# A new order for the first head pair's steps in an attention + two-layer feed-forward kernel on one core

## Chip, cores and metric

One core of one Trainium2 chip runs the kernel. The metric is device time in microseconds (us) of one execution, median over runs. Times inside the execution are counted from the start of the profiled span.

## What is computed

The inputs are q, k, v of 2 batches, 8 heads, 768 positions and head size 64 in float32, two integers (`n_global` = 8, `n_local` = 96), and the weights of two feed-forward layers. The reference, cut to what matters:

```python
scores = (q @ k.T) / sqrt(64)                       # per batch and head
rel = pos[:, None] - pos[None, :]
keep = (pos[None, :] < n_global) | ((rel >= 0) & (rel < n_local))
dist = where(is_global & ~is_local, n_local, abs(rel))
scores = where(keep, scores - slope[h] * dist, -1e9)
a = softmax(scores)                                 # over the keys
x = (a @ v) laid out as [1536, 512]
x = leaky_relu(x @ w_in) @ w_out                    # 512 -> 2048 -> 512
out = rational(x @ w_in2) @ w_out2                  # (a0+a1h+a2h^2+a3h^3)/(1+|b0 h|+|b1|h^2)
```

## The kernel before

Most keys are masked out, so a block of 128 queries needs only its own block of keys, the block before it and the first 32 keys (the "slot", `prep_slots`, replaces the first 32 columns of the block before). Work is cut into **units**: one block of queries of one head. A head **pair** (two heads, stacked in the 128 partitions) has 12 units; unit u has block i = u // 2 and head j = u % 2. There are 8 pairs, so 96 units. Every matmul operand is split into a high and a low float32r part (`kh`/`kl`, `qh`/`ql`), so a score takes three matmuls: kh with qh, kl with qh, kh with ql.

The steps of a unit are: `scores` on TensorE into one half of a PSUM bank (`score_banks[j]`, half i % 2); `least` on VectorE (bias added, minimum taken, result `sn` and `st`); `exp` on ScalarE (`pr`); `transposes` on TensorE into `pt` (two buffers); `evacuate` on ScalarE or VectorE (`pts`); `values` on TensorE. The loop over n (line 638) writes them out by hand as a software pipeline: at n it issues scores and leasts of n, `exp` of n - 1, transposes and evacuation of n - 3, values of n - 5, and then `fillers(n)`. From n = 8 on the scores of four units are issued together every fourth n. The order of every engine is the order of this code (`manual_schedule`); each engine takes its instructions strictly in that order and waits at semaphores.

Fillers prepare the next pair. `prep_k` and `prep_q` are generators that run one step for each n: transposes on TensorE into a bank (line 324); then ScalarE takes the high part of k (line 334) or a scaled copy of q (362); then VectorE takes k's low part (336), and GpSimd splits q (364, 365); then GpSimd copies the slots (352). The banks come from `ffn.bank()`, a pool of **two** that are used in turn (line 682); a transpose into a bank waits until all that read its last contents are done. `PREP0` (line 57) says at which n these generators start during the first pair: k half 0 at 4, q half 0 at 5, k half 1 at 8, q half 1 at 9.

The first pair has its own generators q0, k0 (blocks 0 and 1) and q1, k1 (blocks 2 to 5), `prep_first_q` and `prep_first_k`, since nothing runs before them. Dummy matmuls (`keep_busy`, line 531) run on TensorE ahead of and between its first steps; `BUSY` holds their numbers. The window bias (`window_bias`) is built at the same time: for block 0 (`first`, 128 columns) and for the other blocks (256 columns), by `far` (a comparison on VectorE, then the first 32 columns), `near` and `half` (the second head's slope). Two integers read from memory (`read_ints`) are spread over the partitions by a matmul (`spread`) into `nums`.

`load_v` loads v twice: `vc` in blocks of 128, and `vp`, the same values shifted by one block with the first 32 rows replaced by the first 32 keys (three DMAs per head, on the queue of SyncE). The loads of pairs 0 and 1 stand at lines 550 to 553.

Of the kernel before, what the change touches and what calls it, by code (L numbers as in the profile page):

```python
# [8 lines left out]
F32 = mybir.dt.float32  # L9
# [3 lines left out]
AF = mybir.ActivationFunctionType  # L13
# [4 lines left out]
P = 128  # L18
# [3 lines left out]
EPS_Q = 1.0 + 1e-6  # L22
FAR = 2.56e11


@with_exitstack
def attention_moe_moe2(
# [28 lines left out]

    PREP0 = (("prep_k", 4, 0), ("prep_q", 5, 0), ("prep_k", 8, 1), ("prep_q", 9, 1))
    PREP = (("prep_k", 0, 0), ("prep_q", 1, 0), ("prep_k", 4, 1), ("prep_q", 6, 1))
# [5 lines left out]
    FIRST = 8  # L64
    BUSY = (12, 3, 8)
    XOUT_LAST = (2, 8)
# [26 lines left out]
    intf = cpool.tile([1, 4], F32, name="intf")  # L93
    num1 = cpool.tile([1, 2], F32, name="num1")
    ones = cpool.tile([1, P], F32, name="ones")
    nums = cpool.tile([P, 2], F32, name="nums")
    n_loc = nums[:, 0:1]
# [5 lines left out]
    def read_ints():  # L103
        nc.vector.tensor_copy(intf, ints)
        lo, hi = (intf.rearrange("p (j w) -> p j w", w=2)[:, :, w] for w in range(2))
        nc.vector.scalar_tensor_tensor(hi, lo, 0.0, hi, ALU.is_lt, ALU.add)
        nc.vector.scalar_tensor_tensor(num1, hi, 4294967296.0, lo, ALU.mult, ALU.add)

# [112 lines left out]
    def window_bias(bpool, rpool):  # L221
# [17 lines left out]
        def part(first):  # L239
            return slice(W2, BW) if first else slice(0, W2)  # L240

        def far(first):
            cs = part(first)
            nc.vector.tensor_scalar(mask[:, cs], dist[:, cs], n_loc, FAR, ALU.is_ge, ALU.mult)
            gs = slice(cs.start, cs.start + GW)
            nc.vector.scalar_tensor_tensor(mask[:, gs], col, n_glo, mask[:, gs], ALU.is_ge, ALU.mult)

# [10 lines left out]

        return bias, far, near, half

    def attention(wpool, w1, ffn):
        with ExitStack() as actx:
# [26 lines left out]
            class Pair:  # L289
# [20 lines left out]
                def load_v(self, heads=(0, 1)):  # L310
                    b, h0 = self.b, 2 * self.hp
                    self.vc, self.vp = v_places[self.n % 2]
                    for j in heads:
                        vs = v[b, h0 + j].rearrange("(i p) d -> p i d", p=P)
                        nc.sync.dma_start(self.vc[:, j, :, 0:D], vs)
                        nc.sync.dma_start(self.vp[GW:P, j, :, 0:D], vs[GW:P, 0 : NB - 1])
                        nc.sync.dma_start(
                            self.vp[0:GW, j, :, 0:D], v[b, h0 + j, 0:GW].unsqueeze(1).to_broadcast([GW, NB - 1, D])
                        )

                def transposed(self, raw, s):
# [210 lines left out]

            keep_busy(BUSY[0])
            bias, bias_far, bias_near, bias_half = window_bias(bpool, rpool)
            next(q0)
            read_ints()
            spread = ps.tile([P, W2], F32, tag="pt", name="spread")[:, 0:2]
            nc.tensor.matmul(spread, ones, num1, start=True, stop=True)
            next(k0)
            keep_busy(BUSY[1])  # L540
            next(q0)
            next(k0)
            nc.vector.tensor_copy(nums, spread)
            bias_far(True)
            next(q0, None)
            next(k0)
            next(k0, None)
            bias_near(True)
            bias_half(True)
            P_[1].load_k()  # L550
            P_[0].load_v((0,))
            P_[1].load_q()
            P_[0].load_v((1,))

# [32 lines left out]
            def fillers(n):  # L587
# [29 lines left out]
                for u in AHEAD_STEPS.get(n, ()):  # L617
                    ffn.h_step(u)
                if n == 0:
                    start(k1)  # L620
                    start(q1)
                if n == 1:
                    bias_half(False)
                for g in new:
# [5 lines left out]
            LV = 5  # L630
            GROUPS = {m: (m,) for m in range(0, FIRST, 2)}
            GROUPS.update({m: (m, m + 2) for m in range(FIRST, len(U), 4)})

            LEASTS = {m: (m, m + 1) for m in range(0, FIRST, 2)}
            for m in range(FIRST, len(U), 4):
                LEASTS[m], LEASTS[m + 1] = (m, m + 1), (m + 2, m + 3)
            n = 0
            while n < len(U) or running or n <= len(U) + LV + 1:

                for m in GROUPS.get(n, ()):  # L640
                    for _ in zip(unit(m).scores(), unit(m + 1).scores()):
                        pass
                    if n == 2:
                        keep_busy(BUSY[2])
                for m in LEASTS.get(n, ()):
                    unit(m).least()
                    if m == 1:
                        bias_far(False)
                        bias_near(False)
                for m in (0, 1) if n == 1 else (n - 1,):  # L650
                    if n != 2 and unit(m):
                        unit(m).exp()
                if unit(n - 3):
                    unit(n - 3).transposes()
                    unit(n - 3).evacuate()
                if unit(n - LV):
# [489 lines left out]
```

## Time and profile before

| | us |
|---|---|
| median of 3 runs (637.2 to 637.66) | 637.21 |
| the profiled execution | 637.13 |
| its span, first to last instruction | 635.3 |
| TensorE busy in the span | 626.5 |
| VectorE / ScalarE / GpSimd busy | 469.1 / 439.1 / 206.9 |

The attention takes the first 109 us or so, the feed-forward layers the rest. A row of a timeline gives the start, the duration, engine, line, operation, output and inputs with their shapes, and in brackets how long the engine was idle before it and what released it. Durations on TensorE, VectorE and ScalarE contain a fixed part that overlaps with the next instruction, so the distance from one start to the next is shorter than the duration.

### The profile page before, as it was taken

To read this page: it belongs to the slowest core of one execution; us is meant where nothing else is said; L and a number is where in the kernel's file an instruction comes from. 1 tells how busy PE (TensorE), PEld (TensorE's weight loads), DVE (VectorE), ACT (ScalarE), POOL (GpSimd) and SP (SyncE) were. 2 spreads that over 40 slices of the span, in tenths; PEclk is the share of its full clock that TensorE was granted. 3 is DMA by queue.
4 is the path that set the end of the run, shared out by engine and by line. 5 is a ranking of instruction groups with operands and counts; after the bars stand their busy time and mean duration, and the time that the engine had idled before them with its cause. 6 is when DMAs were issued, how large, how long until landed. Compare 5 with 4: busy or idle time off the path is not lost.

```text
span 635.3 us, 9655 instructions
## 1 busy us (share of the span) xinstructions
PE 626.5 (99%) x3289; PEld 527.7 (83%) x3289; DVE 469.1 (74%) x931; ACT 439.1 (69%) x831; POOL 206.9 (33%) x221
## 2 busy tenths in 40 slices
PE   8999999999999999999999999999999999999996
PEld 7999998888888888888888888888888888888884
DVE  6888888878877545456444489998777777897785
ACT  6888988768776545455444377876677888876672
POOL 3978864443443434341000012222222222112220
PEclk9999999999999999999999999999999999999999
DMA  9987742955267776765322301000033331100002
GB/s 185 222 176 174 165 113 71 311 183 182 81 200 224 229 225 202 245 191 194 99 91 90 91 29 34 1 1 1 0 102 97 101 96 48 68 21 1 2 1 72
DMA packets 80895, 73.34 MB, mean 115 GB/s; under 512 B 50948, under 2 KB 67332, under 8 KB 80836
## 3 DMA queue, kind: packets, MB, share of 16 engines
q1 hardware_dynamic: 80048, 71.12, 39.5%
q0 software_dynamic: 224, 0.92, 0.4%
q8 instruction: 28, 0.46, 0.3%
q10 hardware_dynamic: 564, 0.59, 0.3%
q14 instruction: 31, 0.25, 0.1%
HBM read 60.69 MB, written 11.93 MB: 114 GB/s over the span
## 4 chain that ended last, share of the span: by engine, by line
PE 97%; DVE 2%; ACT 0%; issue 0%; DVEq 0%
PE h L691 41%; PE y L815 21%; PE y L813 21%; PE pt L476 3%; PE sc L440 3%; PE o L498 3%; PE o L497 2%; PE h L324 1%; PE h L209 1%; PE idle L531 0%; PE o L495 0%; DVE sn L451 0%; DVE xl L215 0%; DVE ql L415 0%; DVE kl L402 0%
## 5 line engine op out<-in xcount | busy, mean ns | idle before, releaser
L691 PE MATMUL h<-xh,w 128*128 128x512 f32 x768 | 253.4, 390 | 0.0
L691 PEld LDWEIGHTS h<-xh,w 128*128 128x128 f32 x768 | 144.1, 188 | 29.8
L691 PE MATMUL h<-xl,w 128*128 128x512 f32 x384 | 149.4, 389 | 0.0
L746 POOL TENSOR_TENSOR gl<-u,gh 128x512 fp32r<-128x512 f32 x44 | 57.0, 1296 | 264.4 <-PE y L815 125.4
L813 PE MATMUL y<-gh,w 128*128 128x512 f32 x384 | 126.1, 389 | 0.0
L815 PE MATMUL y<-w,gh 128*128 128x512 f32 x384 | 125.6, 389 | 0.0
L164 POOL TENSOR_TENSOR dec<-dec,wraw 128x512 int32<-128x512 int32 x48 | 63.6, 1334 | 82.7 <-DVE wraw L151 76.3
L813 PEld LDWEIGHTS y<-gh,w 128*128 128x128 f32 x384 | 72.1, 188 | 15.1
L815 PEld LDWEIGHTS y<-w,gh 128*128 128x128 f32 x384 | 72.1, 188 | 15.0
L691 PEld LDWEIGHTS h<-xl,w 128*128 128x128 f32 x384 | 72.2, 188 | 14.5
L815 PE MATMUL y<-w,gl 128*128 128x512 f32 x192 | 75.1, 391 | 0.0
L813 PE MATMUL y<-gl,w 128*128 128x512 f32 x192 | 74.7, 389 | 0.0
L716 DVE TENSOR_TENSOR gl<-h,gh 128x512 fp32r<-128x512 f32 x48 | 33.0, 688 | 51.9 <-ACT gh L715 51.9
L715 ACT ACTIVATE gh<-h 128x512 fp32r<-128x512 f32 x48 | 28.6, 596 | 59.5 <-PE y L813 53.4
L768 ACT ACTIVATE h<-h 128x512 f32<-128x512 f32 x48 | 28.7, 597 | 52.2 <-PE h L691 52.1
L711 DVE SCALAR_TENSOR_TENSOR h<-h,g 128x512 f32<-128x512 f32 x48 | 33.3, 694 | 26.0 <-ACT g L710 25.7
L756 DVE SCALAR_TENSOR_TENSOR w<-w,epsq,h 128x512 f32<-128x512 f32 (+1 forms) x49 | 36.4, 744 | 21.0 <-ACT h L780 20.4
L710 ACT ACTIVATE g<-h 128x512 f32<-128x512 f32 x48 | 28.7, 598 | 30.0 <-PE h L691 29.7
L465 ACT ACTIVATE pr<-sn,st 128x256 f32<-128x256 f32 (+1 forms) x96 | 47.3, 495 | 0.6 <-DVE st L451 0.5
L770 DVE SCALAR_TENSOR_TENSOR w<-h,coef,w 128x512 f32<-128x512 f32 x48 | 35.9, 749 | 16.0 <-ACT w L769 15.8
L815 PEld LDWEIGHTS y<-w,gl 128*128 128x128 f32 x192 | 36.0, 188 | 8.5 <-POOL gl L746 1.1
L813 PEld LDWEIGHTS y<-gl,w 128*128 128x128 f32 x192 | 36.0, 188 | 7.4
(126 smaller groups left out, 1119.2 us busy)
## 6 DMA issues: line engine op xcount, KB each, us to landing
wraw<-in_moe_w_in_dram SPq DMA_DIRECT2D x24, 512.0 KB, 4.6
wraw<-in_moe_w_out_dram SPq DMA_DIRECT2D x24, 512.0 KB, 4.6
scratch<-dec SPq DMA_DIRECT2D x32, 256.0 KB, 5.3
wf<-scratch SPq DMA_DIRECT2D x16, 512.0 KB, 3.5
w<-in_moe_w_in_dram SPq DMA_DIRECT2D x8, 512.0 KB, 4.3
w<-in_moe_w_out_dram SPq DMA_DIRECT2D x8, 512.0 KB, 5.3
vc<-in_v_dram SPq DMA_DIRECT2D x16, 192.0 KB, 3.2
qkraw<-in_q_dram SPq DMA_DIRECT2D x6, 512.0 KB, 3.6
```

The source lines that it names most:

```text
L164: nc.gpsimd.tensor_tensor(ti, ti, self.c, ALU.add)
L465: nc.scalar.activation(self.pr[:, :w], self.sn[:, :w], AF.Exp, bias=self.least_at, scale=-1.0,)
L691: nc.tensor.matmul(h, wt[:, m, c * P : (c + 1) * P], xs[:, c, cs], start=c == 0 and n == 0, stop=c == NK - 1 and n == 2,)
L710: nc.scalar.activation(g, h, AF.Copy)
L711: nc.vector.scalar_tensor_tensor(h, h, 0.01, g, ALU.mult, ALU.max)
L716: nc.vector.tensor_tensor(gl, h, gh.bitcast(F32), ALU.subtract)
L746: (nc.gpsimd if on_pool else nc.vector).tensor_tensor(gl, g, gh.bitcast(F32), ALU.subtract)
L756: nc.vector.scalar_tensor_tensor(ow[:, cs], ow[:, cs], epsq, oh2[:, cs], ALU.add, ALU.mult)
L768: nc.scalar.activation(h2, h, AF.Square)
L770: nc.vector.scalar_tensor_tensor(w0, h2, coef[:, 7:8], w0, ALU.mult, ALU.add)
L813: nc.tensor.matmul(ys[d], wt[:, m, ds_], gs, start=st, stop=sp)
L815: nc.tensor.matmul(ys[d], gs[:, ds_], wt[:, m, :], start=st, stop=sp)
```

## The change

The first pair's steps, up to n = 5, leave the loop and are written out in a new order. The transposes of k0 come before `spread`. The second halves k1 and q1 start between the first score matmuls, the scores of units 2, 3 and of 4, 5 follow one another, and the leasts of 2 to 5 come after both. The mask `far` becomes one `Relu` on ScalarE, (dist + 1 - n_local) * 2^38 cut at zero, and the first 32 columns are a step of their own (`glob`) on VectorE. All of the first pair's v is loaded before pair 1's k and q; for this pair the shifted copy is not loaded but copied from `vc` by GpSimd (`copy_v`). Pair 1's first k and q halves start at n = 6 and 7 instead of 4 and 5. The dummies become 16, 3, 3, 5 and 3 instead of 12, 3 and 8.

```diff
-FAR = 2.56e11
+FAR = 2.0**38
...
-    PREP0 = (("prep_k", 4, 0), ("prep_q", 5, 0), ("prep_k", 8, 1), ("prep_q", 9, 1))
+    PREP0 = (("prep_k", 6, 0), ("prep_q", 7, 0), ("prep_k", 8, 1), ("prep_q", 9, 1))
...
-    BUSY = (12, 3, 8)
+    BUSY = (16, 3, 3, 5, 3)
...
+        nc.vector.tensor_scalar(num1[:, 2:3], num1[:, 0:1], -FAR, FAR, ALU.mult, ALU.add)
...
         def far(first):
-            cs = part(first)
-            nc.vector.tensor_scalar(mask[:, cs], dist[:, cs], n_loc, FAR, ALU.is_ge, ALU.mult)
-            gs = slice(cs.start, cs.start + GW)
-            nc.vector.scalar_tensor_tensor(mask[:, gs], col, n_glo, mask[:, gs], ALU.is_ge, ALU.mult)
+            cs = slice(W2, BW) if first else slice(GW, W2)
+            nc.scalar.activation(mask[:, cs], dist[:, cs], AF.Relu, bias=nums[:, 2:3], scale=FAR)
+
+        def glob(first):
+            if first:
+                m = mask[:, W2 : W2 + GW]
+                nc.vector.scalar_tensor_tensor(m, col, n_glo, m, ALU.is_ge, ALU.mult)
+            else:
+                nc.vector.tensor_scalar(mask[:, 0:GW], col, n_glo, FAR, ALU.is_ge, ALU.mult)
...
-                        nc.sync.dma_start(self.vp[GW:P, j, :, 0:D], vs[GW:P, 0 : NB - 1])
+                        if self.n > 0:
+                            nc.sync.dma_start(self.vp[GW:P, j, :, 0:D], vs[GW:P, 0 : NB - 1])
...
+                def copy_v(self, j):
+                    for r in (slice(GW, 2 * GW), slice(2 * GW, P)):
+                        d = self.vp[r, j, :, 0:D]
+                        z = zeros[r].unsqueeze(1).to_broadcast([r.stop - r.start, NB - 1, D])
+                        nc.gpsimd.tensor_tensor(d, self.vc[r, j, 0 : NB - 1, 0:D], z, ALU.add)
...
             next(q0)
+            next(k0)
             read_ints()
...
             nc.tensor.matmul(spread, ones, num1, start=True, stop=True)
-            next(k0)
             keep_busy(BUSY[1])
             next(q0)
             next(k0)
+            next(q0, None)
             nc.vector.tensor_copy(nums, spread)
+            next(k0)
             bias_far(True)
-            next(q0, None)
-            next(k0)
             next(k0, None)
+            bias_glob(True)
             bias_near(True)
             bias_half(True)
+            P_[0].load_v()
             P_[1].load_k()
-            P_[0].load_v((0,))
             P_[1].load_q()
-            P_[0].load_v((1,))
...
-                if n == 0:
-                    start(k1)
-                    start(q1)
-                if n == 1:
-                    bias_half(False)
...
-            n = 0
+            begun = together(0)
+            next(begun)
+            next(k1)
+            list(begun)
+            next(q1)
+            next(k1)
+            bias_far(False)
+            unit(0).least()
+            unit(1).least()
+            list(together(2))
+            next(q1)
+            next(k1)
+            next(k1, None)
+            next(q1, None)
+            unit(0).exp()
+            unit(1).exp()
+            bias_glob(False)
+            bias_near(False)
+            bias_half(False)
+            for step, _ in enumerate(together(4)):
+                if step == 0:
+                    keep_busy(BUSY[2], P // 2)
+            for m in range(2, 6):
+                unit(m).least()
+            P_[0].copy_v(0)
+            P_[0].copy_v(1)
+            n = 3
...
                 if unit(n - 3):
                     unit(n - 3).transposes()
+                    if n in (4, 5):
+                        keep_busy(BUSY[n - 1], P // 2)
                     unit(n - 3).evacuate()
```

## Rows read from the trace of the kernel before

**Rows 1.** The page's chain that ended last, shares of the span by engine.
```profile
PE 97%; DVE 2%; ACT 0%; issue 0%; DVEq 0%
```
**Rows 2.** TensorE per microsecond: us, busy (instructions), granted clock, DMA share, GB/s.
```profile
10.00:11.00 1.00, 0.76 (x4) 1.00 1.32 220
...
13.00:14.00 1.00, 1.00 (x11) 1.00 1.37 209
```
**Rows 3.** Timeline of TensorE, the dummies and the first transposes.
```profile
3.85 0.41 PE L531 MATMUL idle<-warm 128*128 128x256 f32 x1
4.06 0.63 PE L383 MATMUL h<-ident,qr 128*128 128x128 f32 x2
5.11 0.44 PE L383 MATMUL h<-ident,kr 128*128 128x128 f32 x2
...
8.64 1.22 PE L531 MATMUL idle<-warm 128*128 128x256 f32 x8
```
**Rows 4.** Timeline of ScalarE in the first pair.
```profile
5.58 0.38 ACT L400 ACTIVATE kh<-h 128x256 fp32r<-128x256 f32 x1 [0.47 <-PE h L383]
...
8.11 0.58 ACT L400 ACTIVATE kh<-h 128x512 fp32r<-128x512 f32 x1
...
10.01 0.28 ACT L482 ACTIVATE pts<-pt 128x128 f32<-128x128 f32 x1
```
**Rows 5.** Timeline of VectorE in the first pair.
```profile
7.17 0.29 DVE L451 CUSTOM_DVE_ANT_0 sn<-sc,bias 128x128 f32<-128x128 f32 x1
...
8.27 0.48 DVE L250 SCALAR_TENSOR_TENSOR bias<-dist,nums,mask 128x256 f32<-128x256 f32 x1
8.90 0.42 DVE L451 CUSTOM_DVE_ANT_0 sn<-sc,bias 128x256 f32<-128x256 f32 x1
...
10.46 0.68 DVE L415 SCALAR_TENSOR_TENSOR ql<-h,qh 128x512 fp32r<-128x512 f32 x1
```
**Rows 6.** Instructions by line and shape in 0 to 20 us: busy, mean ns | idle before.
```profile
L465 ACT ACTIVATE pr<-sn,st 128x128 f32<-128x128 f32 x2 | 0.7, 395 | 0.3 <-DVE st L451 0.3
L244 DVE TENSOR_SCALAR mask<-dist,nums 128x128 f32<-128x128 f32 x1 | 0.3, 286 | 0.0
L413 ACT ACT_TABLE_LOAD x1 | 1.3, 1283 | 2.1 <-issue 2.1
```
**Rows 7.** Timeline of TensorE from unit 4's scores to unit 12's.
```profile
11.20 0.39 PE L440 MATMUL sc<-kh,ql 64*128 64x256 f32 x2 [0.21 <-DVE ql L415]
...
13.13 0.38 PE L440 MATMUL sc<-kh,qh 64*128 64x256 f32 x2
...
14.84 0.39 PE L440 MATMUL sc<-kh,qh 64*128 64x256 f32 x2
...
16.41 0.50 PE L324 MATMUL h<-ident,kr 128*128 128x128 f32 x3
...
19.29 0.28 PE L440 MATMUL sc<-kh,ql 64*128 64x128 f32 x2
```
**Rows 8.** The chain that ended last, in order of time, around 12.6 us.
```profile
12.56 0.12 issue
```
**Rows 9.** Timeline of VectorE around unit 8's least.
```profile
14.48 0.55 DVE L336 TENSOR_TENSOR kl<-h,kh 128x384 fp32r<-128x384 f32 x1
...
15.85 0.42 DVE L451 CUSTOM_DVE_ANT_0 sn<-sc,bias 128x256 f32<-128x256 f32 x1 [0.49 <-PE sc L440]
```
**Rows 10.** Timeline of GpSimd, preparation of pair 1.
```profile
15.11 0.97 POOL L352 TENSOR_TENSOR kl<-kl,zeros 128x288 fp32r<-128x288 f32 x2 [0.76 <-DVE kl L336]
16.04 0.83 POOL L364 TENSOR_TENSOR qh<-qt,zeros 128x384 fp32r<-128x384 f32 x1
16.95 1.00 POOL L365 TENSOR_TENSOR ql<-qt,qh 128x384 fp32r<-128x384 f32 x1
```
**Rows 11.** Timelines of GpSimd and VectorE where both read SBUF.
```profile
25.14 1.34 POOL L365 TENSOR_TENSOR ql<-qt,qh 128x384 fp32r<-128x384 f32 x1
...
24.78 0.83 DVE L151 SCALAR_TENSOR_TENSOR wraw<-wraw 128x512 int32<-128x512 int32 x1
```

More of the change, by code (lines that the diff above doesn't have):

```diff
@@ L93, in attention_moe_moe2 @@
     intf = cpool.tile([1, 4], F32, name="intf")
-    num1 = cpool.tile([1, 2], F32, name="num1")
+    num1 = cpool.tile([1, 3], F32, name="num1")
     ones = cpool.tile([1, P], F32, name="ones")
-    nums = cpool.tile([P, 2], F32, name="nums")
+    nums = cpool.tile([P, 3], F32, name="nums")
     n_loc = nums[:, 0:1]
@@ L106, in read_ints @@
         nc.vector.scalar_tensor_tensor(hi, lo, 0.0, hi, ALU.is_lt, ALU.add)
-        nc.vector.scalar_tensor_tensor(num1, hi, 4294967296.0, lo, ALU.mult, ALU.add)
+        nc.vector.scalar_tensor_tensor(num1[:, 0:2], hi, 4294967296.0, lo, ALU.mult, ALU.add)
+        nc.vector.tensor_scalar(num1[:, 2:3], num1[:, 0:1], -FAR, FAR, ALU.mult, ALU.add)
     coef = cpool.tile([P, 8], F32, name="coef")
@@ L257, in half @@
                 nc.scalar.activation(bias[:, 1, cs], bias[:, 0, cs], AF.Copy, scale=0.5)
-        return bias, far, near, half
+        return bias, far, glob, near, half
     def attention(wpool, w1, ffn):
@@ L533, in attention @@
             keep_busy(BUSY[0])
-            bias, bias_far, bias_near, bias_half = window_bias(bpool, rpool)
+            bias, bias_far, bias_glob, bias_near, bias_half = window_bias(bpool, rpool)
             next(q0)
+            next(k0)
             read_ints()
-            spread = ps.tile([P, W2], F32, tag="pt", name="spread")[:, 0:2]
+            spread = ps.tile([P, W2], F32, tag="pt", name="spread")[:, 0:3]
             nc.tensor.matmul(spread, ones, num1, start=True, stop=True)
-            next(k0)
             keep_busy(BUSY[1])
@@ L630, in attention, with together @@
             LV = 5
-            GROUPS = {m: (m,) for m in range(0, FIRST, 2)}
+            GROUPS = {m: (m,) for m in range(6, FIRST, 2)}
             GROUPS.update({m: (m, m + 2) for m in range(FIRST, len(U), 4)})
-            LEASTS = {m: (m, m + 1) for m in range(0, FIRST, 2)}
+            LEASTS = {m: (m, m + 1) for m in range(6, FIRST, 2)}
             for m in range(FIRST, len(U), 4):
                 LEASTS[m], LEASTS[m + 1] = (m, m + 1), (m + 2, m + 3)
-            n = 0
+            def together(m):
+                return zip(unit(m).scores(), unit(m + 1).scores())
+            begun = together(0)
[25 more added lines that the diff above has]
+            n = 3
             while n < len(U) or running or n <= len(U) + LV + 1:
                 for m in GROUPS.get(n, ()):
-                    for _ in zip(unit(m).scores(), unit(m + 1).scores()):
+                    for _ in together(m):
                         pass
-                    if n == 2:
-                        keep_busy(BUSY[2])
                 for m in LEASTS.get(n, ()):
                     unit(m).least()
[L647 to L652, printed above, removed]
+                if unit(n - 1):
+                    unit(n - 1).exp()
                 if unit(n - 3):
                     unit(n - 3).transposes()
+                    if n in (4, 5):
+                        keep_busy(BUSY[n - 1], P // 2)
                     unit(n - 3).evacuate()
```

## The prediction

> **What bounds the kernel now.** I read the chain of work first: 97% of the span is TensorE [rows 1], so an edit counts only by what it does to TensorE's own order. Then TensorE's busy time by microsecond: up to 13 us it has holes (0.76 us of work between 10 and 11), from 13 us on it is full, at a granted clock of 1.00 [rows 2]. So all that the change can give or take lies ahead of some point near 14 us, and behind that point each microsecond of delay is passed on whole to the end. My mark is the start of the first grouped score run, unit 8, at 14.84 [rows 7]. From there both kernels give TensorE the same list. The new time is the old one, plus the shift of this mark, plus any wait that is new behind it.
>
> In the timelines of single engines I then looked for what TensorE waits for ahead of the mark. The last real wait is for ql of the second q half, which VectorE does from 10.46 to 11.14 and which releases the score matmuls at 11.20 [rows 5, 7]. A shorter stop follows at 12.56, 0.12 us in the chain under "issue", ahead of pair 1's first q transposes [rows 8]: nothing on an engine, so by elimination their load.
>
> **The dummies.** The twelve run 0.21 us apart (3.85 to 4.06), as 256 columns do at 1.2 GHz; eight later ones take 1.22 us, 0.13 apart, the 2.4 GHz level [rows 3]. Four more ahead of the first transposes cost 4 x 0.21 = 0.84, or 4 x 0.13 = 0.52 if the clock has risen by then. I take 0.84, since two transposes that start at 4.06 still take 0.63 where two at 5.11 take 0.44 [rows 3]. The q transposes start at 4.90 and end at 5.34.
>
> **First halves.** ScalarE's qh follows at 5.36 and kh about 0.3 behind it. With 0.38 for kh [rows 4] kh is done at 6.03; before it was done at 5.58 + 0.38 = 5.96 [rows 4], since k's transposes stood behind `spread`. So what the dummies cost, the new place of `spread` pays back: level within 0.1. The mask moves to ScalarE: 0.395 by the nearest row with 128 columns (an exponential with a pointer bias) against 0.286 on VectorE [rows 6], two handovers more, and `nums` is copied behind ql. I get the first least at 7.57 instead of 7.17 [rows 5]. `num1`'s third column is one tiny VectorE step, 0.2 at most, hidden by the dummies.
>
> **Second halves.** Their k transposes start behind the first two score matmuls at 6.47 and take some 0.6, so kh of four blocks starts on ScalarE at 7.10 instead of 8.11 [rows 4]. The 224-column Relu, about 0.47, stands between it and qh, which waits for its own transposes until 8.1 in any case. Then ql takes 8.72 to 9.40 instead of 10.46 to 11.14 [rows 5]. This is the gain of the change: the scores of units 4 and 5 are complete at 9.6 instead of 11.6, 2 us earlier.
>
> **Where it goes.** The second bias is now queued behind kl and ql on VectorE. `near` of 256 columns started at 8.27 and takes 0.48 [rows 5]; now it starts at 9.52 and ends at 10.0, or 10.15 with the contention below. Unit 2's least starts at 10.0 to 10.2 instead of 8.90 [rows 5]. ScalarE then does half, the exponential of unit 2, and only behind it unit 0's evacuation: 10.9 to 11.05 instead of 10.01 [rows 4]. It takes 0.28, and the third transposes need the `pt` buffer that it frees, so they start at 11.2 to 11.4. The five dummies lie inside this wait and are free. The three behind the transposes (0.13 each, 0.4) are on the path, and so are unit 0's values. Scores of unit 6 start at 12.35 to 12.5 instead of 13.13 [rows 7]: 0.7 ahead, the stop at 12.56 [rows 8] included.
>
> From there to the mark it was 14.84 - 13.13 = 1.71 [rows 7]. Now pair 1's first k and q transposes lie in this stretch as well; three of them last 0.50 [rows 7], of which some 0.17 overlaps with what follows, so 0.33 each and 0.66 for both. The mark comes to 12.43 + 1.71 + 0.66 = 14.80, a shift of -0.04. The bounds are wide: -0.5 with a clock that rises early and no contention, +0.6 with a late bias.
>
> **Behind the mark: a bank.** The transposes of pair 1 take two banks in turn. Before, k half 0 used one at n = 4 and k half 1 came back to it at n = 8. Now k half 0 uses it at n = 6. Its last reader is VectorE's kl, two steps after the start, so at n = 8, and k half 1's transposes are issued in that same n = 8, right behind it. On VectorE kl stands behind the leasts of units 8 and 9. Unit 8's least started at 15.85, which is 1.01 behind the mark, when the whole grouped run was done [rows 7, 9]; two leasts 0.35 apart bring kl to mark + 1.70; it takes 0.55 [rows 9], so the bank is free at mark + 2.25, with the handover 2.31. TensorE is there at 16.41 - 14.84 = mark + 1.57 [rows 7]. New wait: 0.74, with nothing to hide it, since TensorE keeps its order. Queued behind it are all of TensorE's later steps. If least waited only for its own unit's matmuls, it would be 0.35 shorter; 0.4 is my lower end.
>
> GpSimd says nearly the same in another way: pair 1's kl slots, qh and ql take 0.97 + 0.83 + 1.00 and stood in one unbroken line from 15.11 to 17.95, ahead of their use at 19.29, mark + 4.45 [rows 7, 10]. Behind a kl that ends at mark + 2.25 they end at mark + 5.1. So if the bank didn't hold TensorE, ql would, for about 0.6. The two don't add: with the bank's 0.74 the use moves to mark + 5.2.
>
> **Moved under cover.** The loads: SyncE now issues v first; for pair 1's q that is 464 KB instead of 352 KB ahead, 112 KB at 220 GB/s [rows 2], 0.5 us later than its 12.6, some 0.4 to 1.0 before its use at 14.4. If that cover is gone, each tenth is paid at n = 7. The two shifted loads (120 KB each) that are left out make later transfers earlier, and none of those is waited for behind 14 us, where TensorE is full [rows 2]. `copy_v`: four GpSimd instructions of 320 columns, about 0.7 each between the rows of 288 + 96 and 384 columns [rows 10], 2.8 us from 8.7 to 11.5; unit 2's values want them near 14, and GpSimd's next work comes at 14.6.
>
> **Contention.** `copy_v` runs while `near` reads two operands from SBUF. In this trace GpSimd's ql takes 1.34 beside a VectorE step with two SBUF operands (24.78, 0.83) and 1.00 elsewhere [rows 10, 11]: 0.34 more. I put half of that, 0.15, on `near`; the ends are 0 and a whole copy, 0.7. The Trainium skill's page "SBUF — State Buffer", section "SBUF: two separate sides", says that VectorE and GpSimd share a port pair which one of them holds for its whole instruction while the other blocks. By that rule `near` could wait out a whole copy and the time would be that of the second rival; the 0.34 above shows a part of one only.
>
> **Sum.** 637.13 (the profiled execution, span 635.3 and 1.8 around it) - 0.04 + 0.74 = 637.83; the median lies 0.08 above the profiled one, so 637.9.
>
> **Rivals.** *The front gains more.* If the second bias were no bound (a least of unit 2 not much later than before), the third transposes could follow the dummies at 10.8 and the mark would come at 14.2; with the shorter wait of 0.4 that is 637.13 - 0.6 + 0.4 = 636.9, and 636.3 if neither bank nor GpSimd held anything. For it speaks the 2 us gained on ql; against it that ScalarE takes unit 2's exponential ahead of the evacuation in program order. Even this stays inside 0.2%.
>
> *Slower.* GpSimd's copies hold `near`: from the point where `near` starts inside a copy (8.7 to 11.5, and it starts at 9.5) and waits for its end, 0.55 more than I put. ScalarE's half, unit 2's exponential and all behind follow, and the mark shifts by +0.5; with the bank 637.13 - 0.04 + 0.55 + 0.74 + 0.1 = 638.5. For it speaks the 1.34 [rows 11]; against it that this is a third of what it would need.
>
> *The Relu brings a table.* The trace has one table load, 1.28 [rows 6], ahead of the attention; if Relu needed another, one more would stand ahead of unit 0's exponential and 0.9 of it would reach the mark: 638.8. No row of before has a Relu. The skill's page "ScalarE: Activation LUTs", section "Table sets", says that cheap functions such as relu are in every set; by that there is no second load and 637.9 stands.
>
> **Chances.** Forecast (bank wait with a mark near 14.8): 0.60, 637.4 to 638.4. Front gains more: 0.20, 636.3 to 637.3. Copies hold `near`: 0.16. Table: 0.04. A measurement of this kernel can tell about 0.2%, 1.27 us, from no change. Faster by more than that needs the mark below 13.6 with no wait behind it: 0.06. Slower than 638.48: most of the last two cases and the upper edge of the first, 0.18. The rest, 0.76, is within. The range runs from 636.5 to 638.7.
>
> **What would show it.** In the new profile: q's first transposes at 4.9 and kh done near 6.0; ql of the second half near 9.4; unit 2's least after 10; the third transposes released by ScalarE's evacuation near 11.3; unit 8's scores between 14.3 and 15.4; and then pair 1's second k transposes (line 324's loop) idle for 0.4 to 0.75, released by VectorE's kl. No such idle time would say that the bank reasoning is wrong; unit 8's scores before 14 that the bias chain is. A second table load, or `near` over 0.9 us, would name the slow rivals. The forecast falls if the time leaves 636.5 to 638.7.

## The result and the profile after

| | before | after |
|---|---|---|
| median, us | 637.21 | 642.27 |
| lowest to highest of eight executions | 636.53 to 638.35 | 639.16 to 643.52 |
| the profiled execution | 637.13 | 642.23 |
| its span | 635.3 | 640.4 |

The change costs 5.1 us: the ratio after to before is 1.0074 (95% interval 1.0057 to 1.0091). The forecast was 637.9 in a range of 636.5 to 638.7, a loss of 0.7 that could not be told from no change. The measured loss is seven times as large and lies outside the range.

TensorE in the new profile, first the steps that the prediction named (start us, duration us, engine, line, operation, shapes; in brackets the idle time before it and what released it):

```profile
4.91 0.63 PE L396 MATMUL h<-ident,qr 128*128 128x128 f32 x2
5.33 0.63 PE L396 MATMUL h<-ident,kr 128*128 128x128 f32 x2
...
10.37 0.46 PE L489 MATMUL pt<-ident,pr 128*128 128x128 f32 x2
10.76 0.85 PE L544 MATMUL idle<-warm 64*128 64x256 f32 x5
12.57 0.53 PE L489 MATMUL pt<-ident,pr 128*128 128x128 f32 x2 [0.96 <-ACT pts L495]
13.03 1.01 PE L544 MATMUL idle<-warm 64*128 64x256 f32 x3
...
18.91 0.58 PE L453 MATMUL sc<-kh,qh 64*128 64x256 f32 x2
...
19.68 0.28 PE L453 MATMUL sc<-kh,qh 64*128 64x256 f32 x2
...
21.48 0.55 PE L337 MATMUL h<-ident,kr 128*128 128x128 f32 x3 [0.52 <-ACT qt L375]
...
24.13 0.33 PE L453 MATMUL sc<-kh,qh 64*128 64x128 f32 x2
```

The mark, unit 8's scores, stands at 18.91 and not at 14.84 [rows 7]: +4.07. Unit 12's first scores follow at 24.13, 5.22 behind the mark, where before they came 4.18 behind it, at 19.02:

```profile
19.02 0.33 PE L440 MATMUL sc<-kh,qh 64*128 64x128 f32 x2
```

That makes +1.04, and 4.07 + 1.04 = 5.11 is the whole loss. Everything happens ahead of 25 us. Look at the durations as well: three dummies take 1.01 at 13.03, and a score run that takes 0.39 in [rows 7] takes 0.58. From 19.68 on they are short again.

The view by stretch shows why (columns as in [rows 2]: length, then busy us of TensorE, its weight loads, VectorE, ScalarE and GpSimd, then the granted clock, the DMA share and GB/s):

```profile
11.50:12.00 0.50, 0.11 (x1) 0.00 (x0) 0.50 (x3) 0.34 (x2) 0.44 (x2) 1.00 1.39 218
12.00:12.50 0.50, 0.00 (x0) 0.00 (x0) 0.50 (x5) 0.50 (x3) 0.50 (x1) 1.00 1.39 219
12.50:12.70 0.20, 0.13 (x1) 0.13 (x2) 0.20 (x1) 0.20 (x2) 0.08 (x1) 1.00 1.39 218
12.70:12.90 0.20, 0.20 (x2) 0.07 (x2) 0.14 (x2) 0.20 (x2) 0.00 (x0) 0.71 1.41 216
12.90:13.40 0.50, 0.50 (x2) 0.37 (x2) 0.00 (x0) 0.50 (x4) 0.00 (x0) 0.50 1.38 218
...
19.40:19.60 0.20, 0.20 (x6) 0.20 (x6) 0.00 (x0) 0.00 (x0) 0.00 (x0) 0.50 0.33 64
19.60:19.80 0.20, 0.20 (x7) 0.20 (x7) 0.00 (x0) 0.00 (x0) 0.00 (x0) 0.97 0.67 72
```

The granted clock falls to 0.50, the 1.2 GHz level, at about 12.8, right behind the wait of 0.96, and is back at about 19.6. In before it is 1.00 from 10 to 11 and from 13 to 14 [rows 2]. The mean clock of seven of the eight executions of after is .992 or .993; the one at .999 took 639.16.

VectorE and ScalarE tell what lengthened the wait. `near` takes 0.99 where it took 0.48 [rows 5], and ScalarE's `half` waits for it:

```profile
10.24 0.99 DVE L256 SCALAR_TENSOR_TENSOR bias<-dist,nums,mask 128x256 f32<-128x256 f32 x1
...
11.26 0.42 ACT L263 ACTIVATE bias<-bias 128x256 f32<-128x256 f32 x1 [0.82 <-DVE bias L256]
11.84 0.51 ACT L478 ACTIVATE pr<-sn,st 128x256 f32<-128x256 f32 x1 [0.16 <-DVE st L464]
12.26 0.26 ACT L495 ACTIVATE pts<-pt 128x128 f32<-128x128 f32 x1
...
9.45 3.13 POOL L332 TENSOR_TENSOR vp<-vc,zeros 32x320 f32<-32x320 f32 x4
```

The second of these four copies, read by itself (GpSimd's timeline from 10.3 to 10.4 us), starts just ahead of `near`:

```profile
10.22 0.73 POOL L332 TENSOR_TENSOR vp<-vc,zeros 64x320 f32<-64x320 f32 x1
```

### The profile page after: what moved, and what is told of

It reads as the page before. It is cut to its first block, busy times and chain, and to the rows that moved or that the text cites. A ratio compares the mean times of both kernels' runs of the same rounds, so it can differ in the third digit from the quotient of the medians.

```text
span 640.4 us, 9674 instructions
## 1 busy us (share of the span) xinstructions
PE 631.2 (99%) x3296; PEld 531.5 (83%) x3296; DVE 471.0 (74%) x930; ACT 439.5 (69%) x833; POOL 209.6 (33%) x225
## 4 chain that ended last, share of the span: by engine, by line
PE 97%; DVE 2%; ACT 0%; issue 0%; DVEq 0%; ACTq 0%
PE h L725 41%; PE y L849 21%; PE y L847 20%; PE pt L489 3%; PE sc L453 3%; PE o L511 3%; PE o L510 2%; PE h L337 1%; PE idle L544 1%; PE h L210 1%; PE o L508 0%; DVE sn L464 0%; PE h L396 0%; DVE xl L216 0%; DVE bias L256 0%
## 5 line engine op out<-in xcount | busy, mean ns | idle before, releaser
L464 DVE CUSTOM_DVE_ANT_0 sn<-sc,bias 128x256 f32<-128x256 f32 (+1 forms) x96 | 33.9, 396 | 12.5 <-PE sc L453 12.4
```

The lines of the kernel that those rows point to most:

```text
L464: nc.vector.tensor_tensor_reduce(self.sn[:, :w], self.sc[:, :w], bias[:, self.j, b0 : b0 + w], self.pair.slope, 3.0e38, ALU.add, ALU.min, ...
```

## The experiments

The new profile left two theories of the fall. A: the wait of 0.96 alone makes it. B: the dummies between the steps, which the change puts on 64 rows (`keep_busy(..., P // 2)`), hold the clock less than the 128-row dummies of before. The rest were the terms of my sum: copies, bank, dummies, order. In each comparison the kernel before ran beside it, with medians of 637.26 to 637.55.

### e1: the shifted v loaded, no copies by GpSimd

```diff
-                        if self.n > 0:
-                            nc.sync.dma_start(self.vp[GW:P, j, :, 0:D], vs[GW:P, 0 : NB - 1])
+                        nc.sync.dma_start(self.vp[GW:P, j, :, 0:D], vs[GW:P, 0 : NB - 1])
...
-            P_[0].copy_v(0)
-            P_[0].copy_v(1)
```

> The changed kernel, but the first pair's shifted copy of v is loaded by DMA as before and GpSimd copies nothing. In the changed kernel the bias step near (VectorE, 10.24) took 0.99 us beside GpSimd's copies where it took 0.48 before, TensorE then stood idle for 0.96 us, and the granted clock fell to 1.2 GHz from 12.8 to 19.6 us. Theory A (the copies lengthen the wait and the wait drops the clock): near takes 0.5, the third transposes start at about 12.0, the idle time falls to some 0.4, the clock stays at 2.4 GHz, and the time is 642.3 - 3.4 - 0.5 = 638.4. Theory B (the clock falls because TensorE had long had little work on all 128 rows, whatever the wait): near takes 0.5 as well, but the clock still falls and the time is 641.8.

Median 639.0, ratio to before 1.0036 (1.0018 to 1.0054). Four of ten executions, at clocks of .992 to .994, took 640.9 to 642.3; the six at .997, most of them 637.9 to 638.4. In the profile (one of the four):

```profile
9.98 0.48 DVE L256 SCALAR_TENSOR_TENSOR bias<-dist,nums,mask 128x256 f32<-128x256 f32 x1
...
11.80 0.44 PE L488 MATMUL pt<-ident,pr 128*128 128x128 f32 x2 [0.40 <-ACT pts L494]
```

Without the copies `near` is back at 0.48, and the third transposes come 0.77 earlier. The wait of 0.40 is less than half of 0.96, and the clock still falls in four of ten. So the fall doesn't need the copies; that it is rarer without them (4 of 10 against 7 of 8) fits their part in the wait.

### e2: the later dummies on 128 rows

```diff
-                    keep_busy(BUSY[2], P // 2)
+                    keep_busy(BUSY[2])
...
-                        keep_busy(BUSY[n - 1], P // 2)
+                        keep_busy(BUSY[n - 1])
```

> The changed kernel with its last eleven dummies on 128 rows instead of 64; nothing else. Their columns and their time are the same, so the waits stay as they are (near 0.99, idle 0.96). Theory A (the wait drops the clock): it falls as before, 642.3. Theory B (the half-filled array counts too little): it stays at 2.4 GHz, and the time is 642.3 - 3.4 = 638.9.

Median 639.68, ratio 1.0026 (1.0009 to 1.0042). No clock is below .997, where seven of the eight executions of after are at .992 or .993; the two kernels differ by the rows alone. But the profiled execution took 642.2 with another fault: its matmuls last as at the 1.2 GHz level from the start until about 17 us, although the record shows 1.00 throughout. So this profile can't show whether the wait matters; e7 can.

### e3: pair 1's first preparation at steps 4 and 5 again

```diff
-    PREP0 = (("prep_k", 6, 0), ("prep_q", 7, 0), ...
+    PREP0 = (("prep_k", 4, 0), ("prep_q", 5, 0), ...
```

> The changed kernel with pair 1's first k and q halves started at n = 4 and 5 again instead of 6 and 7. My bank theory: the wait of 0.52 us ahead of pair 1's second k transposes (21.48, released by VectorE's kl) is gone, 641.75 if the clock falls all the same. Theory A on the clock: three transposes at n = 4 stand where TensorE was idle, the idle time falls to some 0.5 to 0.6, and the clock may stay: then about 638.4. Theory B: six full transposes come ahead of the fall and it could stay too, so this run tells the bank's price by the wait itself and by its profile, not by its time. Rival to the bank: k's load lands too late for n = 4 and TensorE waits there for 0.5 instead.

Median 638.36, ratio 1.0012 (1.0002 to 1.0021), ten executions from 637.6 to 639.0, no fall, and no wait for the bank.

```profile
11.74 0.55 PE L337 MATMUL h<-ident,kr 128*128 128x128 f32 x3
12.78 0.44 PE L489 MATMUL pt<-ident,pr 128*128 128x128 f32 x2 [0.49 <-ACT pts L495]
```

Three transposes on 128 rows now stand at 11.74, inside the wait, which is 0.49. The dummies are still on 64 rows and the copies still hold `near` for 0.99. So this one line takes 3.9 of the 5.1 us away: it removes the bank wait and fills the hole. It also limits theory B. Half rows alone make no fall here, while e1, with a wait of 0.40 and no transposes in it, has four in ten: what TensorE does in the hole matters beside the rows of the dummies.

### e4: the reverse in the kernel before

```diff
-    PREP0 = (("prep_k", 4, 0), ("prep_q", 5, 0), ...
+    PREP0 = (("prep_k", 6, 0), ("prep_q", 7, 0), ...
```

> The kernel before with one thing of the change: pair 1's first k and q halves start at n = 6 and 7. My bank theory: TensorE waits 0.5 to 0.75 us ahead of pair 1's second k transposes for VectorE's kl, the stop of 0.1 to 0.3 for pair 1's q load goes, and the time is 637.2 + 0.3 to 0.7 = 637.5 to 637.9 with the clock at 2.4 GHz throughout. If the bank costs nothing: 637.0 to 637.2.

Median 639.02, ratio 1.0027 (1.0015 to 1.0038), no fall. The profile has the bank wait alone, at full clock:

```profile
15.21 0.39 PE L440 MATMUL sc<-kh,qh 64*128 64x256 f32 x2
...
17.47 0.55 PE L324 MATMUL h<-ident,kr 128*128 128x128 f32 x3 [0.52 <-ACT qt L362]
...
20.13 0.33 PE L440 MATMUL sc<-kh,qh 64*128 64x128 f32 x2
```

The row names ScalarE's qt as what ended the wait, and the prediction had named VectorE's kl. In after, where the wait ends at 21.48, the two are:

```profile
20.93 0.55 DVE L349 TENSOR_TENSOR kl<-h,kh 128x384 fp32r<-128x384 f32 x1
...
20.94 0.48 ACT L375 ACTIVATE qt<-h 128x384 f32<-128x384 f32 x1
```

They end 0.06 apart, kl at 21.48 and qt at 21.42, so the rows hardly part them. In the kernel's order the bank of pair 1's second k transposes is the one that its first k half used, which kl reads and qt does not. In e4 the bank is free at mark + 2.26, where the prediction said + 2.31. From mark to unit 12's scores it is 4.92 instead of 4.18: the wait costs 0.74, of which the row shows 0.52, since idle time is counted from the modelled end of the matmul before. The mark is 0.37 later as well, and 637.13 + 0.37 + 0.74 = 638.24 comes near the profiled execution's 638.08. The median lies 0.9 above that one; what makes the difference is not settled.

### e5: half rows in the kernel before

```diff
-                        keep_busy(BUSY[2])
+                        keep_busy(BUSY[2], P // 2)
```

> The kernel before with its eight later dummies (8.64 us) on 64 rows instead of 128; their columns, their time and all waits stay. Theory A (a wait of TensorE drops the clock): no wait is longer than before, so the clock stays and the time is 637.3. Theory B (what counts is how much of the array works): some runs fall to 1.2 GHz from about 10 to 13 us on, for up to 6.8 us as in the changed kernel, and come out at 639 to 640.7; the median is 637.3 to 639, by how many fall.

Median 638.16, ratio 1.0016 (1.0002 to 1.0029). Five of ten executions have clocks of .994 or .995, and take 638.1 to 638.5; of the 101 executions of the unchanged kernel that ran beside these experiments none is below .996. The dummies take nearly as long as on 128 rows, where the eight took 1.22 [rows 3]:

```profile
8.58 1.11 PE L531 MATMUL idle<-warm 64*128 64x256 f32 x8
```

No wait was added, no order changed: half the rows of eight dummies are enough to lower the mean clock in half of the executions. I read these as falls; where they lie no profile shows, since the profiled execution (636.83) is one without. Two more, at .997, took 640.3 and 640.5.

### e6: e1, e2 and e3 together

> The changed kernel with three parts put back: the shifted v loaded by DMA, all dummies on 128 rows, pair 1's first halves at n = 4 and 5. Kept are the new order of the first pair's steps, 16 first dummies, the mask on ScalarE and v first. If copies, rows and bank are the whole loss, the clock stays in every run, no wait for VectorE's kl is left, and the time is that of the front alone: by my walk the mark then came 0.7 earlier than before, 636.6 to 637.3. If the front itself loses (the first transposes behind 16 dummies, which the two profiles put at 4.9 instead of 4.06, and the second bias behind kl and ql): 637.8 to 638.4, with unit 8's scores at 15.3 to 15.9 instead of 14.84.

Median 638.99, ratio 1.0024 (1.0014 to 1.0034): 0.6 above e3 alone by the medians, though the two intervals overlap. The profile shows a new wait:

```profile
13.02 0.52 PE L336 MATMUL h<-ident,kr 128*128 128x128 f32 x3 [1.09 <-DMA kr<-in_k_dram]
...
14.82 0.52 PE L336 MATMUL h<-ident,qr 128*128 128x128 f32 x3 [0.54 <-DMA qr<-in_q_dram]
```

With v, now with its shifted part, ahead of pair 1's k and q, and with their use moved forward, both loads are late by 1.09 and 0.54. In e3, which has the same early preparation with v first but copies the shifted part, neither wait stands. So early preparation together with the loaded shifted part needs the load order of before.

### e7: 12 first dummies and 128 rows

```diff
-    BUSY = (16, 3, 3, 5, 3)
+    BUSY = (12, 3, 3, 5, 3)
```

and the edit of e2.

> The changed kernel with all dummies on 128 rows and 12 first dummies instead of 16. First transposes at 4.06 again. Against the same kernel with 16 (median 639.7): if the four dummies only delay, 0.5 to 0.8 less, 638.9 to 639.2. If they are what lets the clock rise early (it rose only at about 17 us in the profile of the kernel with full rows and 16), the rise comes late in more runs and the time goes up to 640 to 642. The profile also tells, where the clock is up, whether an idle time of near 1 us with full rows drops it: theory A says yes, theory B no.

Median 638.65, ratio 1.0023 (1.0009 to 1.0038), no fall in ten executions by their clocks of .997 and .998. One of the ten took 642.12 at .998, as long as the profiled execution of e2; no profile shows why. The profile kept is the one that refutes theory A:

```profile
9.84 1.00 DVE L256 SCALAR_TENSOR_TENSOR bias<-dist,nums,mask 128x256 f32<-128x256 f32 x1
...
12.18 0.44 PE L489 MATMUL pt<-ident,pr 128*128 128x128 f32 x2 [0.90 <-ACT pts L495]
...
15.45 0.39 PE L453 MATMUL sc<-kh,qh 64*128 64x256 f32 x2
...
17.71 0.55 PE L337 MATMUL h<-ident,kr 128*128 128x128 f32 x3 [0.52 <-ACT qt L375]
...
20.37 0.33 PE L453 MATMUL sc<-kh,qh 64*128 64x128 f32 x2
```

The wait is 0.90, nearly the 0.96 of after, and matmuls behind it are short. In the 2.5 us ahead of the third transposes TensorE was busy for 1.60 us in this kernel and for 1.54 in after: the same filling, on 128 rows here and on 64 there.

### e10: 12 first dummies, half rows

The edit of `BUSY` alone, so that e10 and e7 differ by the rows and nothing else.

> The kernel after with one edit, 12 first dummies instead of 16; the later ones stay on 64 rows. It differs from the earlier run with 12 dummies on full rows, whose clock held over a wait of 0.90 for the third transposes, by the rows alone. Theory (work on 64 rows does not keep the clock up): the granted clock falls to 0.50 near 12 to 13 us in most runs, their clocks at .992 to .995, median 641.0 to 642.0. Rival (the four more dummies or their late clock made the fall, the rows did not): no fall, clocks at .997 or more, median 638.3 to 638.9.

Median 641.91 over four executions, ratio 1.0069 (1.0054 to 1.0084). Three have clocks of .991 or .992 and take 641.8 to 642.0; the profiled one, 643.87, had the late clock of e2 instead, with its matmuls long until 20.5 us. So three of four fell by their clocks (no profile shows where), and of e7 none in ten. With after and e2 these are two pairs of kernels that differ by the rows alone, and in both the fall goes with the half rows. The medians are 3.3 us apart here and 2.6 there. The rows are shown to decide it in this order of steps; that they do so only together with the hole is what e3 adds.

### e8: all parts back but the order and the mask

e7 with the edits of e1 and e3 and with the loads in the order of before:

```diff
-            P_[0].load_v()
             P_[1].load_k()
+            P_[0].load_v((0,))
             P_[1].load_q()
+            P_[0].load_v((1,))
```

> The kernel after with five edits: 12 first dummies, the later ones on 128 rows, pair 0's shifted v loaded by DMA again with GpSimd's copies left out, pair 1's first preparation at steps 4 and 5, and the loads issued in the order of before (pair 1's k, v of one head, pair 1's q, v of the other). What is left of the change is the order of the first pair's steps, the joined score runs and the mask on ScalarE. Theory (the cost beside the clock was: GpSimd's copies 0.5, four dummies 0.5 or more, the late preparation 0.5 of bank wait, the late loads 1.1 + 0.5 as in the run with three edits): third transposes near 11.6, no wait for loads, no wait for the bank, no fall of the clock, mark at 14.7 to 15.1, median 637.2 to 637.7. Rival (the new order itself costs, since the second bias stands behind kl and ql): mark at 15.3 to 15.8, median 637.9 to 638.5.

Median 637.39 beside 637.55, ratio 1.0011 (0.9994 to 1.0028): no difference that can be told. Its profile comes near the front of the prediction, with four dummies fewer, no copies and pair 1's first transposes earlier than the prediction had them:

```profile
8.69 0.69 DVE L427 SCALAR_TENSOR_TENSOR ql<-h,qh 128x512 fp32r<-128x512 f32 x1
...
11.39 0.44 PE L488 MATMUL pt<-ident,pr 128*128 128x128 f32 x2
...
12.56 0.52 PE L336 MATMUL h<-ident,qr 128*128 128x128 f32 x3 [0.21 <-issue]
...
14.71 0.39 PE L452 MATMUL sc<-kh,qh 64*128 64x256 f32 x2
...
18.88 0.33 PE L452 MATMUL sc<-kh,qh 64*128 64x128 f32 x2
```

Mark 14.71, with no wait for the bank (4.17 from mark to unit 12). Pair 1's q is waited for at 12.56, the place of the stop before [rows 8]: the 2 us gained on ql end at a load. Three of the twelve executions took 640.9 to 641.4 at clocks of .996 to .999.

### e9: e8 with the second bias ahead of kl and ql

```diff
             unit(1).least()
+            bias_glob(False)
+            bias_near(False)
             list(together(2))
             next(q1)
+            bias_half(False)
...
-            bias_glob(False)
-            bias_near(False)
-            bias_half(False)
```

> The kernel of the run before this one with one more edit: the second bias (the global columns, near, and ScalarE's half) is issued right behind the first two leasts, ahead of kl and ql of the second half. Theory (unit 2's exponential waits for the chain kl, ql, near, half): near starts near 8.4, kl and ql move 0.7 later, to 9.7 and 10.4, unit 2's least follows ql at 10.4 instead of about 10.5 without copies, and no half stands ahead of its exponential: third transposes 0.3 to 0.7 earlier than in the run before, mark at 14.2 to 14.7, median 0.3 to 0.6 lower, 636.7 to 637.3. Rival (ql is then the bound: the scores of units 4 and 5 wait for it, and TensorE's first transposes of unit 0 stand behind them): mark level within 0.2, median level within 0.2.

Median 637.66, ratio 1.0020 (1.0004 to 1.0036). My theory was wrong and its rival right in kind: ql moves to 9.86, TensorE waits 0.21 for it at 10.59, and behind it unit 0's transposes come at 10.94 instead of 10.00; the mark stands at 15.19, 0.48 later. Of this 0.26 is there ahead of the edit, since kh of the second half starts at 7.37 where it started at 7.11 in e8, because this execution's first matmuls stayed long until later; the edit itself is left with some 0.2. Five of the twelve executions took more than 639.5. In both places tried for the second bias, either it or ql is late.

### e11: 16 first dummies in the kernel before

```diff
-    BUSY = (12, 3, 8)
+    BUSY = (16, 3, 8)
```

> The kernel before with one edit, 16 first dummies instead of 12. It prices the first term of the prediction's sum by itself. Prediction's price: the first transposes 0.84 later (4.06 to 4.90), here with spread in its old place, so that nothing pays it back; if all of it goes through to the mark the time is 637.35 + 0.84 = 638.2, with q's and k's first transposes still at 0.63. Rival (the wait for the second half's ql and the stop at 12.56 have slack for it, or the dummies run at the 2.4 GHz level from some point): 637.4 to 637.8.

Median 637.66, ratio 1.0006 (0.9996 to 1.0015). In the profile the first transposes are 0.86 later (4.92), and the second half's ql lets TensorE go at 12.05 instead of 11.20 [rows 7]; the mark is only 0.54 later (15.38). So four dummies are paid at 0.84 up to that wait, as I priced them, and the stop for pair 1's load behind it gives 0.3 back. The median moved by 0.1, less than the profile; the interval reaches from -0.3 to +1.0. One of the ten executions took 639.85.

### e12 and e13: the late clock, and the load of q

e12 is e8 with `spread` between q's and k's first transposes, as in before. e13 is e12 with the shifted v of the first head issued behind pair 1's q (`load_v` gets a second argument, 0 for `vc` and 1 for `vp`). In the cut the lines with `next(k0)` are e12's edit and those with `load_v` are e13's.

```diff
             next(q0)
-            next(k0)
             read_ints()
...
             nc.tensor.matmul(spread, ones, num1, start=True, stop=True)
+            next(k0)
...
-            P_[0].load_v((0,))
+            P_[0].load_v((0,), (0,))
             P_[1].load_q()
+            P_[0].load_v((0,), (1,))
             P_[0].load_v((1,))
```

> The kernel of the run with five edits (12 first dummies, rows full, shifted v loaded, early preparation, loads in the order of before) with one more: the spread matmul stands between q's and k's first transposes again, as in the kernel before. Three of twelve executions of the run without this edit took 640.9 to 641.4 at a clock record of .996 to .999, as an execution takes whose early matmuls last as at the 1.2 GHz level until 17 or 20 us; of the kernel before none in 78 did. Theory (in the new order the clock comes up later and is missed in some executions because the one-row spread matmul, during which TensorE has little work, stands behind k's transposes, next to the dummies): no execution above 639.5, median 637.2 to 637.5. Rival (the late rise comes from the work behind it, with score matmuls on 64 rows between the second halves' transposes, where the kernel before has full transposes and eight dummies together): 2 to 5 of 12 above 639.5, median 637.3 to 638.

> The kernel of the run before this one with one more edit: the loads of pair 0's shifted v (120 KB and 40 KB of the first head) are issued behind pair 1's q instead of ahead of it. TensorE's last wait ahead of the mark in the run with five edits is 0.21 for that q, at 12.56. Theory (q lands 160 KB at some 215 GB/s earlier, 0.7, so that the wait is gone, and the shifted v still lands ahead of unit 2's values at 14.2): q's transposes at 12.3, mark at 14.3 to 14.5, median 0.2 to 0.4 below the run before, 636.8 to 637.2. Rival (the shifted v is then late and TensorE waits for it at unit 2's values, or the load wait only moves to evacuations): mark level within 0.1, median level. It also doubles the sample on the late rise.

e12: median 637.58, ratio 1.0007 (0.9998 to 1.0016); two of eleven executions above 639.5. e13: median 637.6, ratio 1.0014 (1.0001 to 1.0026); two of twelve. The place of `spread` is not what makes the clock late. The profile of e12 is one of the long executions (640.96), that of e13 a short one; up to k's first transposes they are the same to 0.01 us. Of e12, then of e13:

```profile
5.13 0.69 PE L395 MATMUL h<-ident,kr 128*128 128x128 f32 x2
5.47 0.99 PE L543 MATMUL idle<-warm 128*128 128x256 f32 x3
...
12.77 1.42 PE L543 MATMUL idle<-warm 128*128 128x256 f32 x5
...
17.14 0.28 PE L452 MATMUL sc<-kl,qh 64*128 64x256 f32 x2
```

```profile
5.13 0.44 PE L398 MATMUL h<-ident,kr 128*128 128x128 f32 x2
5.33 0.60 PE L546 MATMUL idle<-warm 128*128 128x256 f32 x3
...
10.10 0.84 PE L546 MATMUL idle<-warm 128*128 128x256 f32 x5
...
13.86 0.44 PE L510 MATMUL o<-vc,pts 128*128 128x65 f32 x2 [0.36 <-DMA vc<-in_v_dram]
...
14.84 0.39 PE L455 MATMUL sc<-kh,qh 64*128 64x256 f32 x2
```

By the durations the clock comes up near 17 in e12 and near 5.1 in e13, with the same work on TensorE before. In e13 the wait for q is gone (its transposes come at 12.08 behind their neighbours), and 0.36 for the second head's v takes its place at 13.86: the rival, with the mark 0.13 behind that of e8. In both orders TensorE waits for a load ahead of 14 us; that the loads as a whole are the floor of this front is argued from these two.

## Why the prediction was wrong, point by point

The way from after back to before, one edit or group at a time, by medians:

| kernel | median | step |
|---|---|---|
| after | 642.27 | |
| 12 first dummies (e10) | 641.91 | -0.4 |
| and later dummies on 128 rows (e7) | 638.65 | -3.3 |
| and no copies, preparation at 4 and 5, loads in the old order (e8) | 637.39 | -1.3 |
| before, beside e8 | 637.55 | +0.2 |

The steps depend on the order in which they are taken: with 16 first dummies the rows are worth 2.6 (after to e2) and the four dummies then 1.0 (e2 to e7), and the one line of e3 takes 3.9 by itself.

**The step that failed.** The prediction said of TensorE "From there both kernels give TensorE the same list", and of the dummies that they "lie inside this wait and are free". Both hold at an unchanged clock only. I read the granted clock of 1.00 [rows 2] as a fact of the chip, where it was earned by what TensorE did ahead of it. The diff changes that work in plain sight, `P // 2` rows in eleven dummies, and I priced them by their time alone, which is nearly the same on either number of rows (1.11 and 1.22 for eight). No rival had the clock falling. What the runs showed in its place: with the eleven dummies on 64 rows and a wait of 0.96 for the third transposes, the granted clock goes to 0.50 from 12.8 to 19.6 us. In the profile this is 3.07 up to the mark (from the third transposes to it after takes 18.91 - 12.57 = 6.34, and e7 at full clock 15.45 - 12.18 = 3.27), and 0.30 more behind it (5.22 against e7's 4.92).

**The term that was too small: contention.** I put 0.15 on `near`, with 0 and 0.7 as the ends. It was 0.99 against 0.48, so 0.51, with the copies; 0.48 in e1, e6 and e8, without them. The second rival had this mechanism and nearly this price, and got a chance of 0.16 because I took the 0.34 of another pair of instructions [rows 11] as typical. The Trainium skill's page "SBUF — State Buffer", section "SBUF: two separate sides", says that a VectorE step with two SBUF inputs and a GpSimd step that reads SBUF exclude each other at a shared port for an instruction's length; `near` agrees with that: it starts at 10.24, the copy beside it runs from 10.22 to 10.95, and `near` ends at 11.23, 0.28 behind the copy. The page was nearer than my row.

**The bias chain.** I expected the third transposes at 11.2 to 11.4 and found 12.57. In e8, with 12 dummies and no copies, it is 11.39, and e7 and after tell the rest: 0.51 are the copies, 0.40 the four dummies (`near` starts at 10.24 and 9.84), and the last 0.27 stand between the starts of `near` in e7 and e8 (9.84 and 9.57), whose early matmuls got their clock at different times. "So what the dummies cost, the new place of `spread` pays back" is wrong: kh was done at 6.39, not 6.03, since k's transposes still took 0.63 at 5.33. For q's transposes ahead of it I had put 0.44, the time at the higher clock, right after reading 0.63 for them; qh started at 5.58 and not at 5.36.

**The bank.** Right, and nearly to the hundredth: 0.74 was put, e4 and e7 show 4.92 from mark to unit 12's scores instead of 4.18, and the wait is absent with the early preparation (e3, e6, e8). Whether kl ended it, as I had it, or qt, rests on the kernel's order of banks more than on the rows (e4).

**The gain.** That the second half's ql comes earlier was right in kind (9.31 in after and 8.69 in e8, 8.72 put, 10.46 before), and that this is no gain as well. That the mark of e8, 14.71, lies 0.09 from my 14.80 is in part luck: e8 has four dummies fewer and no copies, and e7, at full clock and with the copies, has its mark at 15.45. **The mask** as a Relu brought no second table ahead of the attention: the 128 columns take 0.41, the 224 columns 0.47, as estimated.

**The sum.** 637.13 - 0.04 + 0.74 = 637.83 against 642.23. The mark was 4.11 later than I had it: 1.27 at the third transposes, 3.07 from the clock, -0.23 since the way from there to the mark was shorter than I put. Behind the mark 0.74 for the bank and 0.30 for the slow rest: 637.13 - 0.04 + 4.11 + 0.74 + 0.30 = 642.24.

**Still open.** Why the clock comes up late in some executions, 3.5 us longer, although the record shows 1.00. Above 639.5 there are 12 of 47 executions of e8, e9, e12 and e13, and none of the 101 of before (highest 639.21). e12 leaves the place of `spread` out as the cause. Before has eight 128-row dummies in a block at 8.64 [rows 3], which the new order lacks; that they catch a late clock would fit the two executions of e5, with that block on 64 rows, at 640.3 and 640.5. Against it stands the 639.85 of e11, which has the block on 128 rows. This is argued and not shown. Open as well is what picks the executions that fall: four of ten in e1, and five of ten in e5, where no wait was added. No version beat the kernel before.

## What to carry to other kernels

Dummy matmuls are priced by the clock that they hold, not by their time: when a change alters their number, their rows or the hole that they fill, put "the granted clock falls here" among the rivals, with (duration at 1.2 GHz less duration at 2.4 GHz) of the stretch behind as its price. A copy moved to GpSimd is not free when a VectorE step with two SBUF operands on the critical chain starts beside it; here it cost 0.51. And when a chain is shortened by 2 us, look for the next thing that arrives at a fixed time, here a load at 12.56, before the gain is counted.

## What the hardware showed that I had not expected

Eight dummies on 64 instead of 128 rows, of nearly the same length (1.11 against 1.22 us), lowered the mean granted clock in five of ten executions of the kernel before (e5), and with the same busy time around a wait of 0.9 the clock fell on 64 rows and held on 128 (after against e7). Three transposes on 128 rows in that wait kept it up too, with the dummies still on 64 (e3).

The record of the granted clock can show 1.00 where the matmuls last as at 1.2 GHz: in e12 five dummies on 128 rows take 1.42 at 12.77, where in e13 the same five take 0.84 at 10.10, and both records show 1.00 there. Nor does it show the first rise, at about 5 us in before, where two transposes take 0.63 at 4.06 and 0.44 at 5.11 [rows 3]. The Trainium skill's page "TensorE: Matmul & The Clock Gate", section "Seeing it yourself", warns that the clock events of a trace have been seen to be unreliable; these rows agree, and durations of one shape are the safer view.
